# Loading the first token tiles as column halves over two queues, and q matmuls of the third token tile ahead of the first k matmuls

## The chip, the cores and the metric

The kernel runs on one core of one Trainium2 chip. Times are device microseconds (us), the median of several executions. "Span" is the time of the profiled execution from its first to its last instruction, about 1.7 us less than the run's time. PE is the TensorE matmul, PEld its weight load, DVE is VectorE, ACT ScalarE, POOL GpSimd, SP SyncE (here only an issuer of DMAs).

## The reference, cut to what matters

```python
x = A_x                                   # 1 x 2048 x 512, bf16
xn = _layernorm(x, axis=-1)               # 16 token tiles of 128 rows
return x + _A_ref(xn, A_wqkv, A_wo) + _B_ref(xn, B_w_in, B_w_sp, B_b_sp, B_w_out)
```

`_A_ref` is an attention over 8 dilated positions whose q, k, v come from `xn @ wqkv`; `_B_ref` is a gated MLP with a 2048 x 2048 mixing of the tokens. Everything starts from the normalised x, transposed so that the 512 channels lie on the partitions (`xnT`). Until the first tiles are loaded, normalised, transposed and copied, PE has nothing useful to do.

## The kernel before

The 16 token tiles are numbered 4 * tb + j. The first four to be worked on are tiles 0, 4, 8, 12 (j = 0); the text calls them **tile 0, 1, 2, 3** of the head. The loads, and the helpers:

```python
    def load_x0(E, tb, p0=0, p1=P):
        E.dma_start(xall[p0:p1, 0, tb, :], x2[tb * TBS + p0:tb * TBS + p1, :])
    ...
    load_x0(SP, 0, 0, 64)                 # tile 0: two partition halves
    load_x0(A, 0, 64, P)
    load_x0(A, 1)                         # tile 1: whole, on ACT's queue
    G.dma_start(xall[:, 0, 2:4, :], xblk[0][:, 2:4, :])     # tiles 2 and 3, by POOL
    load_wqk(SP, 0)                       # q weights
    SP.dma_start(xall[:, 1], xblk[1])     # x block 1
    load_wqk(SP, 1)                       # k weights
    ...
    def ln_stats(i):
        j, tb = i % 4, i // 4
        V.bn_stats(stats[:, i, :], xall[:, j, tb, :])
        V.bn_aggr(mv[:, i, :], stats[:, i, :])
    ...
    def qk_part(pq, j, m, b0, b1, ccs=(0, 1), p0=None):
        ...
        for cc in ccs:
            for kc in range(C):
                PE.matmul(pq[:, cc, ...], wqk[:, sd, kc, c0 + cc:D:C],
                          xv[:, kc, b0:b1, j, :], start=(kc == 0), stop=(kc == C - 1))
```

The head's schedule (order is by hand, each engine runs its instructions in the order written):

```python
    warm_up(10)                           # matmuls on zeros
    for n in range(2):
        ln_stats(t0[n]); ln_sqrt(col(t0[n]))
    for n in range(2):
        ln_tile(t0[n])                    # 1/x, then (x - mean) * rstd on DVE
        tr_copy(t0[n], tr(t0[n]))         # PE transposes into PSUM, ACT copies to xnT
    warm_up(1)
    warm_up(1, 2)
    ...                                   # statistics and normalisation of tiles 2, 3
    qk_part(pqs[0], 0, 0, 0, 2)           # q of tiles 0, 1
    tr_copy(t0[2], tr(t0[2]))
    qk_part(pqs[1], 0, 1, 0, 2, (0,))
    tr_copy(t0[3], tr(t0[3]))
    qk_part(pqs[1], 0, 1, 0, 2, (1,))
    qk_part(pqs[2], 0, 2, 0, 2)           # the first of k
```

The last group of output rows (o = 3) adds 16 x 4 matmuls of attention, eight row groups of 24-row matmuls on the tail channels of `uT`, and then the full ones:

```python
    def u_tr(n):                          # the last of 16: "T14", from SP
        SP.dma_start_transpose(uT[:, (n // 4) % 2, :, (n % 4) * P:(n % 4 + 1) * P], z1u[:, n % NZ1, :])
    ...
    def out_rest(o):                      # needs all four uT of its group
        for rt in range(2):
            for tb in range(TB):
                ...
                    PE.matmul(pc, uT[q:q + KR, o % 2, m, tb * P:(tb + 1) * P], wout[q:q + KR, m, cs], ...)
```

## Time and profile before

| | value |
|---|---|
| time | 204.58 us median of 3 (204.37 to 204.71) |
| span, granted clock | 202.8 us, 0.998 |
| PE busy | 97% |
| share of PE in the chain that ended last | 85% |
| first useful matmul (q) | 7.47 us |
| landings: tile 0, tile 1, tiles 2 and 3, q weights, x block 1, k weights | 3.35, 4.39, 5.16, 6.67, 8.17, 9.66 us |

The landings are the times of the last of a load's sixteen semaphore increments, from the trace's records.

With PE at 97% one reads where the other 3% are. The chain of waits of the first 10 us, start, length and what it was (SPq and ACTq are issues of DMAs):

```profile
0.81 0.56 ACTq L165
...
1.41 2.98 DMA r_x<-in_A_x_dram
...
4.41 0.71 DVE stats L203
...
5.14 0.18 DVE mv L204
...
5.41 0.42 DVE r_x L214
...
5.88 0.41 PE pt L221 x4
...
6.31 1.12 ACT xnT L225 x2
...
7.47 1.03 PE pq L306 x8
...
8.50 0.40 PE pt L221 x4
8.90 0.44 PE pq L306 x4
```

The reader is to see a single file of dependent steps: tile 1's load, its statistics, aggregation, normalisation of tile 0, transposes, two copies, q. After 7.47 the chain is PE's own work, with one small step: the transposes of tile 2 (8.50), which follow the q matmuls directly in this list, but started when DVE's normalisation ended (8.03 + 0.41), as the DVE timeline shows (start, busy, instruction):

```profile
4.17 0.18 DVE L204 BATCH_NORM_AGGREGATE mv<-stats 128x2 f32<-128x6 f32 x1
4.41 0.69 DVE L203 BATCH_NORM_STATS2 stats<-r_x 128x6 f32<-128x512 bf16 x1
5.14 0.18 DVE L204 BATCH_NORM_AGGREGATE mv<-stats 128x2 f32<-128x6 f32 x1
...
6.25 0.69 DVE L203 BATCH_NORM_STATS2 stats<-r_x 128x6 f32<-128x512 bf16 x1
...
8.03 0.41 DVE L214 TENSOR_SCALAR r_x<-r_x,mv,rstd 128x512 bf16<-128x512 bf16 x1
```

And the PE timeline of the last group's tail channels (L506) and full matmuls (L521):

```profile
194.23 0.38 PE L506 MATMUL po<-r_w,r_uz 24*128 24x512 bf16 x2
194.24 0.38 PE L506 MATMUL pa<-r_w,r_uz 24*128 24x512 bf16 x2
...
195.04 0.59 PE L521 MATMUL po<-r_w,r_uz 128*128 128x512 bf16 x2 [0.16 <-issue]
```

### The profile page before, as it was taken

Reading aid. Unit: us, or ns where it says so; the run is one execution under the profiler, and the core shown is the slowest. Engines: PE = TensorE matmul, PEld = TensorE weight load, DVE = VectorE, ACT = ScalarE, POOL = GpSimd, SP = SyncE. Lnnn points to the kernel's source line nnn. Section 1 sums busy time; section 2 is a strip of 40 time slices with the busy share of each in tenths; the row PEclk is TensorE's granted clock in tenths of the full one; section 3 lists DMA queues with packets and bytes.
Section 4 is the critical chain, followed back from the end, with each engine's and each line's share of the span. In section 5 each row is a group of like instructions: output and inputs, shape, how many; then the busy total and the mean of one; then the engine's idle time right before and its main releaser. Section 6 shows DMA issues by size and latency. Waiting matters only on the chain.

```text
span 202.8 us, 4061 instructions
## 1 busy us (share of the span) xinstructions
PE 196.2 (97%) x1679; PEld 125.0 (62%) x1683; DVE 185.0 (91%) x263; ACT 102.5 (51%) x163; POOL 18.0 (9%) x15
## 2 busy tenths in 40 slices
PE   7799999999999999999999999999999999999993
PEld 2689856555666666666566666666654644664561
DVE  4999799999999999999899999999999999988504
ACT  3575978978999986913733273595230010021000
POOL 5000000799200000000000000000000000000000
PEclk9999999999999999999999999999999999999999
DMA  5973448900000399149950975959910393574453
GB/s 146 353 264 73 96 94 253 198 1 3 0 0 3 87 157 206 44 87 239 220 123 21 204 135 118 231 138 162 207 42 3 97 174 89 140 203 94 116 184 103
DMA packets 65826, 25.91 MB, mean 128 GB/s; under 512 B 56208, under 2 KB 65488, under 8 KB 65552
## 3 DMA queue, kind: packets, MB, share of 16 engines
q1 hardware_dynamic: 65360, 25.12, 56.5%
q10 hardware_dynamic: 368, 0.27, 0.6%
q8 instruction: 13, 0.21, 0.5%
q0 software_dynamic: 80, 0.26, 0.4%
q14 instruction: 5, 0.04, 0.1%
HBM read 10.13 MB, written 2.10 MB: 60 GB/s over the span
## 4 chain that ended last, share of the span: by engine, by line
PE 85%; DMA 4%; SPq 3%; DVE 3%; issue 2%; ACT 1%; ACTq 0%; DVEq 0%
PE pg L449 35%; PE pz L235 19%; PE pq L306 13%; PE pv L410 7%; PE po L521 4%; PE po L497 4%; DMA r_x<-in_A_x_dram 1%; PE pl L360 1%; DMA r_uz<-r_uz 1%; DMA out_dram<-r_qk 1%; SPq L469 1%; DVE r_qk L511 1%; SPq L516 1%; SPq L474 1%; PE pt L221 1%
## 5 line engine op out<-in xcount | busy, mean ns | idle before, releaser
L449 PE MATMUL pg<-z,r_qk 128*128 128x344 bf16 x448 | 67.0, 309 | 0.0
L449 PEld LDWEIGHTS <-r_qk 128*128 128x128 bf16 x448 | 43.8, 98 | 21.8
L235 PE MATMUL pz<-w_z,xnT 128*128 128x344 bf16 x256 | 40.0, 309 | 0.0
L424 DVE TENSOR_TENSOR r_pr<-r_x,r_w 128x2048 bf16<-128x2048 bf16 x32 | 38.3, 1219 | 1.2 <-PE pl L360 0.8
L455 ACT ACTIVATE gs<-pg,b_col 128x688 bf16<-128x688 f32 x16 | 13.3, 830 | 41.3 <-PE pg L449 19.4
L428 DVE TENSOR_TENSOR r_pr<-r_pr 128x2048 bf16<-128x2048 bf16 x28 | 33.8, 1216 | 0.0
L235 PEld LDWEIGHTS <-xnT 128*128 128x128 bf16 x256 | 24.9, 98 | 13.4 <-issue 0.8
L306 PE MATMUL pq<-xnT,r_w 128*128 128x256 bf16 (+1 forms) x176 | 28.5, 316 | 0.3 <-ACT xnT L225 0.3
L340 DVE TENSOR_TENSOR r_pr<-r_qk 128x2048 bf16<-128x2048 bf16 x24 | 28.0, 1215 | 0.0
L306 PEld LDWEIGHTS <-r_w 128*128 128x128 bf16 x184 | 20.2, 114 | 7.5 <-issue 0.5
L297 ACT ACTIVATE r_uz<-pz 128x688 bf16<-128x688 f32 x16 | 11.7, 741 | 20.8 <-PE pz L235 20.6
L634 POOL CAST b_col<-b 128x16 f32<-128x16 bf16 x1 | 15.1, 15142 | 32.7 <-DMA b<-in_B_b_sp_dram 32.7
L316 ACT CAST r_qk<-pq 128x1024 bf16<-128x1024 f32 (+1 forms) x16 | 15.4, 990 | 4.4 <-PE pq L306 4.0
L521 PE MATMUL po<-r_w,r_uz 128*128 128x512 bf16 x66 | 14.9, 379 | 0.6 <-issue 0.6
L511 DVE TENSOR_TENSOR r_qk<-po,r_qk 128x512 bf16<-128x512 f32 x14 | 9.1, 684 | 6.8 <-DMA out_dram<-r_qk 5.1
L497 PE MATMUL po<-r_lg,r_pr 32*128 32x512 bf16 x224 | 14.5, 375 | 0.0
L410 PE MATMUL pv<-xnT,r_w 128*32 128x512 bf16 x256 | 14.4, 380 | 0.0
L521 PEld LDWEIGHTS <-r_uz 128*128 128x128 bf16 x85 | 8.0, 98 | 9.8 <-issue 1.5
L349 DVE TENSOR_TENSOR r_pr<-r_pr 128x4096 bf16<-128x4096 bf16 x6 | 13.6, 2286 | 0.0
L259 ACT ACTIVATE junk<-z 128x688 bf16<-128x688 bf16 x16 | 12.5, 780 | 0.1
L253 ACT ACTIVATE z<-pz 128x688 bf16<-128x688 f32 x16 | 11.7, 738 | 1.5 <-PE pz L235 1.5
L203 DVE BATCH_NORM_STATS2 stats<-r_x 128x6 f32<-128x512 bf16 x16 | 10.8, 672 | 1.7 <-DMA r_x<-in_A_x_dram 1.6
(82 smaller groups left out, 176.1 us busy)
## 6 DMA issues: line engine op xcount, KB each, us to landing
r_qk<-in_A_x_dram SPq DMA_DIRECT2D x16, 128.0 KB, 3.2
r_lg<-in_A_wo_dram SPq DMA_DIRECT2D x8, 256.0 KB, 4.6
out_dram<-r_qk SPq DMA_DIRECT2D x15, 128.0 KB, 1.8
r_w<-in_A_wqkv_dram SPq DMA_DIRECT2D x3, 512.0 KB, 4.6
r_x<-in_A_x_dram SPq DMA_DIRECT2D x3, 512.0 KB, 5.8
w_z<-in_B_w_in_dram SPq DMA_DIRECT2D x2, 688.0 KB, 5.4
r_w<-in_B_w_out_dram SPq DMA_DIRECT2D x1, 640.0 KB, 5.5
r_x<-in_A_x_dram POOLq DMA_DIRECT2D x1, 256.0 KB, 3.9
```

The source lines that it names most:

```text
L235: PE.matmul(pz[:, hh, 0:FHALF], xnT[:, kc, i * P:(i + 1) * P], wz[:, kc, hh * FHALF:(hh + 1) * FHALF], start=(kc == 0), stop=(kc == C - 1))
L306: PE.matmul(pq[:, cc, p0 * P:(p0 + b1 - b0) * P], wqk[:, sd, kc, c0 + cc:D:C], xv[:, kc, b0:b1, j, :], start=(kc == 0), stop=(kc == C - 1))
L316: cast = A.copy(dst, pq[:, :, p0 * P:(p0 + b1 - b0) * P].rearrange("p c (b t) -> p c b t", b=b1 - b0))
L340: prod = V.tensor_tensor(pr[g % 3][:, c].rearrange("p w b t -> p b w t"), q3.unsqueeze(2).broadcast_to([P, TB, 4, P]), k4, ALU.mult)
L349: V.tensor_tensor(pr[g % 3][:, 0:2], pr[g % 3][:, 0:2], pr[g % 3][:, 2:4], ALU.add)
L410: PE.matmul(pv[32 * tb:32 * tb + 32, dd, :], wv[:, kc, 2 * d2 + dd, :], xnT[:, kc, tb * TBS:(tb + 1) * TBS], start=(kc == 0), stop=(kc == ...
L424: V.tensor_tensor(pw_t[n], vp[:, :, off:off + P], a_sb[:, slot_w(w), ts].unsqueeze(1).broadcast_to([P, DH, P]), ALU.mult)
L428: V.tensor_tensor(pw_t[n] if dst is None else dst, pw_t[n], pw_t[m], ALU.add)
L449: PE.matmul(pg[:, hh, 0:FHALF], wsp[n][:, k, :], z2[:, k, hh * FHALF:(hh + 1) * FHALF], start=(k == 0), stop=(k == NT - 1))
L497: PE.matmul(pc, op[32 * tb:32 * tb + 32, d, o * P:(o + 1) * P], wo_r[32 * tb:32 * tb + 32, d, cs], start=(d == 8), stop=False, tile_positi ...
L521: PE.matmul(pc, uT[:, o % 2, m, tb * P:(tb + 1) * P], wout[:, m, cs], start=False, stop=(m == MCH - 3))
L634: G.tensor_copy(b_col[:], b16[:])
```

## The change

Its intent: tiles 0 and 1 come sooner and in column halves, so that statistics start on the first half; the second tile's copy is halved so that the first q matmuls (which take the channels two quarters at a time) start on the first half; and q matmuls of tile 2 fill PE while the k weights, now issued later, are still on their way.

```diff
-    stats = sb.tile([P, NT, 6], F32, name="stats")
+    stats = sb.tile([P, NT, 12], F32, name="stats")
...
-    def load_x0(E, tb, p0=0, p1=P):
-        E.dma_start(xall[p0:p1, 0, tb, :], x2[tb * TBS + p0:tb * TBS + p1, :])
+    def load_x0(E, tb, h):
+        E.dma_start(xall[:, 0, tb, 256 * h:256 * h + 256], x2[tb * TBS:tb * TBS + P, 256 * h:256 * h + 256])
...
-    load_x0(SP, 0, 0, 64)
-    load_x0(A, 0, 64, P)
-    load_x0(A, 1)
+    for tb in range(2):
+        load_x0(SP, tb, 0)
+        load_x0(A, tb, 1)
...
-    def ln_stats(i):
+    def ln_stats(i, parts=1):
         j, tb = i % 4, i // 4
-        V.bn_stats(stats[:, i, :], xall[:, j, tb, :])
-        V.bn_aggr(mv[:, i, :], stats[:, i, :])
+        w = D // parts
+        for h in range(parts):
+            V.bn_stats(stats[:, i, 6 * h:6 * h + 6], xall[:, j, tb, w * h:w * h + w])
+        V.bn_aggr(mv[:, i, :], stats[:, i, 0:6 * parts])
...
     for n in range(2):
-        ln_stats(t0[n])
+        ln_stats(t0[n], 2)
...
-        tr_copy(t0[n], tr(t0[n]))
+    tr_copy(t0[0], tr(t0[0]))
+    pt1 = tr(t0[1])
+    tr_copy(t0[1], pt1, 0, 2)
+    tr_copy(t0[1], pt1, 2, 4)
...
-    qk_part(pqs[0], 0, 0, 0, 2)
+    qk_part(pqs[0], 0, 0, 0, 2, kcs=range(2))
+    qk_part(pqs[0], 0, 0, 0, 2, kcs=range(2, 4))
...
     qk_part(pqs[1], 0, 1, 0, 2, (1,))
+    qk_part(pqs[0], 0, 0, 2, 3)
+    qk_part(pqs[1], 0, 1, 2, 3)
     qk_part(pqs[2], 0, 2, 0, 2)
...
-        qk_part(pqs[n], 0, n, 2, 4)
+        qk_part(pqs[n], 0, n, 3, 4)
```

Instruction by instruction, PE gets 16 weight loads and 16 matmuls more (3,398 instructions for 3,366, counted as twice the weight loads): 16 matmuls of 256 columns became 32 of 128. Nothing else is added but two statistics, one copy and one load.

More of the change, by code (lines that the diff above doesn't have):

```diff
@@ L222, in tr, with tr_copy @@
         return pt
-    def tr_copy(i, pt):
-        A.copy(xnT[:, :, i * P:(i + 1) * P], pt[:])
+    def tr_copy(i, pt, c0=0, c1=C):
+        A.copy(xnT[:, c0:c1, i * P:(i + 1) * P], pt[:, c0:c1, :])
     def tr_dma(i):
@@ L298, in z1_gelu, with qk_part @@
                      tiles.pop(("x", n))[:, :, 0:FHALF], ACT.Gelu_apprx_tanh)
-    def qk_part(pq, j, m, b0, b1, ccs=(0, 1), p0=None):
+    def qk_part(pq, j, m, b0, b1, ccs=(0, 1), p0=None, kcs=range(C)):
         sd, c0 = m // 2, 2 * (m % 2)
@@ L304, in qk_part @@
         for cc in ccs:
-            for kc in range(C):
+            for kc in kcs:
                 PE.matmul(pq[:, cc, p0 * P:(p0 + b1 - b0) * P], wqk[:, sd, kc, c0 + cc:D:C],
```

## The prediction

> **What bounds the kernel now.** One core, granted clock 0.998, median 204.58 us (204.37 to 204.71). The page has PE 97% busy; the chain of waits is 85% PE. From its first projection matmul at 7.47 us the PE runs almost without idle time to about 179 us (timeline). So the change can shorten only the head: the time before 7.47 us, and the gap at 8.34 to 8.50, where the transposes of the third tile wait for the DVE's normalisation. The rest should only slide.
>
> **The head, by the chain and the timeline.** ACT issues tile 1 at 1.41, it lands at 4.39; DVE statistics 4.41, aggregation 5.14, first normalisation 5.41, transposes 5.88, two ACT copies from 6.31 (585 ns each), matmul 7.47. Tile 0 came as two partition halves issued together at 0.81; the semaphore records show them full at 2.97 and 3.35; its statistics ran 3.45 to 4.14. The q weights landed at 6.67, x block 1 at 8.17, the k weights at 9.66, with DMA at about 350 GB/s from 4 us on.
>
> **What the change does.**
> - Loads: four 64 KB column halves, so the first half's statistics run while the second lands. The Trainium skill ("DMA: Bandwidth & Descriptors", Rules for kernel authors) says that transfers to disjoint partition halves serialize; 2.97 and 3.35 agree, and I expect column halves to do likewise. Tile 1 comes ahead of the weights on both queues. Rows shrink from 1024 to 512 bytes: twice the packets, which costs some of the gain.
> - Statistics: two 256-wide instructions instead of one of 690 ns: an estimate of 0.42 us each, starting 0.33 apart (VectorE at 0.96 GHz: the Trainium skill, "Trainium Kernel Development and Optimization", NeuronCore Architecture). With both halves there it costs 0.07 us; with halves apart it saves up to 0.3. My estimate: tile 1's aggregation starts at 4.95 (4.75 to 5.15) instead of 5.14, and normalisations and transposes shift with it.
> - Copy in halves: 372 ns each (estimated from 585 at 512 columns, 1012 at 1024), so the first q matmul could start another 0.2 us earlier, near 7.0. But the q weights are issued 0.6 us later and may land at 6.7 to 7.2, and what is won here waits at the third tile's transposes, which the DVE sets. Little by itself.
> - Order: 16 matmuls of 256 columns (109 ns apart) become 32 of 128 (transposes of that width are 56 ns apart): +0.04 us. They put 0.9 us before the first k matmul, so that later k weights (9.7 to 10.3) don't stall it.
>
> **On the critical path**: 0.2 us off the third tile's transposes (8.50 to about 8.3), kept to the end. Predicted 204.35 us, 80% range 203.9 to 204.8; faster by over 2%: 0.01, within 2%: 0.98, slower: 0.01.
>
> **What would show it.** Tile 0's statistics starting near 3.1; tile 1's aggregation near 4.95; first q matmul at 7.0 to 7.3, PE still waiting for the DVE before the third tile's transposes; k matmuls at about 10.9 without a wait; PE continuous afterwards, every later stage 0.2 earlier.
>
> **What would make it wrong.** The 512-byte rows landing so late that the DVE starts no earlier; q weights landing past 7.3; 128-column matmuls slower than 56 ns apart (their weights are strided: 0.8 us more if they took 80); a later wait (block 1 of x past 8.6, the transposing DMAs) that takes the gain back.

## More of the kernel before

From the page, engine use and the chain by engine (busy us, share, instructions; then shares of the span):

```profile
PE 196.2 (97%) x1679; PEld 125.0 (62%) x1683; DVE 185.0 (91%) x263; ACT 102.5 (51%) x163; POOL 18.0 (9%) x15
...
q8 instruction: 13, 0.21, 0.5%
...
PE 85%; DMA 4%; SPq 3%; DVE 3%; issue 2%; ACT 1%; ACTq 0%; DVEq 0%
```

## The result, and the profile after

The changed kernel took 204.56 us (median of 4, 204.38 to 204.61), the kernel before 204.50 in the same comparison (4 runs): ratio 1.000, 95% interval 0.9983 to 1.0018. The span is 202.9 us for 202.8.

The head did become faster, and by more than forecast at first. The DVE timeline after (the lines that answer to those above):

```profile
2.94 0.75 DVE L205 BATCH_NORM_STATS2 stats<-r_x 128x6 f32<-128x256 bf16 x2 [1.12 <-DMA r_x<-in_A_x_dram]
3.73 0.21 DVE L206 BATCH_NORM_AGGREGATE mv<-stats 128x2 f32<-128x12 f32 x1
3.85 0.70 DVE L205 BATCH_NORM_STATS2 stats<-r_x 128x6 f32<-128x256 bf16 x2
4.58 0.21 DVE L206 BATCH_NORM_AGGREGATE mv<-stats 128x2 f32<-128x12 f32 x1
...
6.07 0.69 DVE L205 BATCH_NORM_STATS2 stats<-r_x 128x6 f32<-128x512 bf16 x1 [0.28 <-DMA r_x<-in_A_x_dram]
...
7.86 0.41 DVE L216 TENSOR_SCALAR r_x<-r_x,mv,rstd 128x512 bf16<-128x512 bf16 x1
```

Tile 1's aggregation starts at 4.58 instead of 5.14, 0.56 us earlier, but tile 2's normalisation at 7.86 only 0.17 us earlier: its statistics waited at 6.07 for the load of tiles 2 and 3, which landed at 6.05 instead of 5.16. PE's side of the same stretch, from the list of waits (waiter, what it waited for, us in total, times, longest):

```profile
PEld L308 <- DMA r_w<-in_A_wqkv_dram: 1.0, 1, 1.0
...
PE pq L308 <- ACT rstd L209: 0.5, 1, 0.5
```

The first q matmul started at 7.36. The second line blames ACT, but ACT's own list has nothing that PE needs then: the weight load just before that matmul waited for the q weights (first line), which landed at 7.32. A matmul and its weight load wait separately, and both lines have to be read.

From 9.3 us on, PE was continuous and 0.14 to 0.18 us earlier than before: the transposes of tile 2 at 8.33 (before 8.50), the first matmul of the MLP at 22.35 (22.49), the first of the token mixing at 76.69 (76.83), the first tail-channel matmul of the last group at 194.09 (194.23). From the PE timelines, the transposes after (8.33) and the first matmuls of the MLP after and before:

```profile
8.33 0.40 PE L223 MATMUL pt<-ident,r_x 128*128 128x128 bf16 x4
...
22.35 3.66 PE L237 MATMUL pz<-w_z,xnT 128*128 128x344 bf16 x24
...
22.49 3.66 PE L235 MATMUL pz<-w_z,xnT 128*128 128x344 bf16 x24
```

In the last group the gain was lost. PE timeline, list of waits, and DMA queues in the stretch 192.0 to 193.6 us (packets, MB, share of 16 engines):

```profile
194.09 0.38 PE L508 MATMUL po<-r_w,r_uz 24*128 24x512 bf16 x2
194.47 0.39 PE L508 MATMUL pa<-r_w,r_uz 24*128 24x512 bf16 x2
...
195.24 0.38 PE L523 MATMUL po<-r_w,r_uz 128*128 128x512 bf16 x1 [0.16 <-issue]
```

```profile
PEld L508 <- DMA r_uz<-r_uz: 0.5, 1, 0.5
```

```profile
q1 hardware_dynamic: 527, 0.22, 59.0%
q8 instruction: 1, 0.02, 4.1%
```

After its first two matmuls the last group waits for a transposing DMA, until 194.47. Before, the same matmuls followed at once (194.24), and the same DMA queues between 192.0 and 193.5 us had no packet of queue 8:

```profile
q1 hardware_dynamic: 658, 0.24, 69.8%
```

(That trace's own last packet of queue 8 began at 193.56, after the DMA had landed.)

The trace's semaphore records tell more of this DMA, the last of the sixteen that transpose u (T14). Its sixteen increments came between 192.89 and 193.03 before. After, fifteen came by 192.89 and the sixteenth at 194.43. The Trainium skill ("DMA: Bandwidth & Descriptors", Why a DMA increments its semaphore by 16 and not by 1) says that each of up to sixteen engines posts one increment when its own data has landed; so one engine of sixteen was 1.5 us late. And a 16,384-byte packet of queue 8 ran from 192.33 to 193.39 us, while T14 was moving. The Trainium skill ("Runtime: NRT & Kernel Launch", Instruction fetch mechanics) says that an engine's sequencer refills its instructions by its own DMA queue in 16 KiB blocks, 256 instructions each. This agrees with that: thirteen such packets in each trace, an estimate of 13 x 256 = 3,328 instructions, beside PE's 3,366, and no other engine has more than a few hundred. That page also calls the cost "mostly hidden". Here it was not, if the following theory holds. There was slack, but not enough: before, T14 had landed at 193.03 and the first matmul that needs it ran at 194.24, 1.2 us later.

**Theory 1.** The change adds 32 PE instructions. They move the blocks in which PE's instructions are fetched, and the last fetch now falls on the last transposing DMA, whose slowest engine then holds up PE for about 0.35 us. That takes the head's gain back. **Rival A:** the late DMA was chance, a matter of that one execution. **Rival B:** it comes with the head's earlier timing or the new loads, not with the number of instructions. Open besides: which part of the change makes the head's gain, and why it was only 0.14 us after 0.56 us at the aggregation.

### The profile page after: what moved, and what is told of

The parts are those of the page before. It is cut to its first block, busy times and chain, and to the rows that moved or that the text cites. A ratio compares the mean times of both kernels' runs of the same rounds, so it can differ in the third digit from the quotient of the medians. Undisturbed runs are those within 1.5% of the kernel's fastest.

```text
span 202.9 us, 4098 instructions
## 1 busy us (share of the span) xinstructions
PE 197.4 (97%) x1695; PEld 125.2 (62%) x1699; DVE 185.3 (91%) x265; ACT 102.6 (51%) x164; POOL 18.0 (9%) x15
## 4 chain that ended last, share of the span: by engine, by line
PE 87%; SPq 3%; DVE 2%; issue 2%; DMA 2%; ACT 1%; DVEq 0%
PE pg L451 35%; PE pz L237 19%; PE pq L308 13%; PE pv L412 7%; PE po L523 4%; PE po L499 4%; PE pwm L550 2%; SPq L476 1%; PE pl L362 1%; DMA r_uz<-r_uz 1%; DVE r_qk L513 1%; SPq L471 1%; DMA out_dram<-r_qk 1%; PE pt L223 1%; SPq L518 1%
## 5 line engine op out<-in xcount | busy, mean ns | idle before, releaser
L308 PE MATMUL pq<-xnT,r_w 128*128 128x256 bf16 (+2 forms) x192 | 28.6, 304 | 0.5 <-ACT rstd L209 0.5
L412 PEld LDWEIGHTS <-r_w 128*32 128x32 bf16 x256 | 9.4, 138 | 4.5 <-issue 0.3
```

The costliest lines, as they stand in the source:

```text
L308: PE.matmul(pq[:, cc, p0 * P:(p0 + b1 - b0) * P], wqk[:, sd, kc, c0 + cc:D:C], xv[:, kc, b0:b1, j, :], start=(kc == 0), stop=(kc == C - 1))
L412: PE.matmul(pv[32 * tb:32 * tb + 32, dd, :], wv[:, kc, 2 * d2 + dd, :], xnT[:, kc, tb * TBS:(tb + 1) * TBS], start=(kc == 0), stop=(kc == ...
```

## The experiments

Twelve runs, timed against the kernel before on the same chip. The kernel before itself was spread over 204.46 to 206.64 us on these chips (single executions over 1 us off the median occurred in it and in two of the variants, shift_only and after_far_act; their cause was not studied).

| run | median us (range, runs) | before on the same chip | ratio (95% interval) |
|---|---|---|---|
| before_again | 204.84 (1) | 204.84 (204.50 to 205.80, 11) | - |
| after_again | 204.36 (204.28 to 204.55, 6) | the same | 0.9974 (0.9955 to 0.9993) |
| shift_only | 205.19 (204.88 to 206.36, 6) | the same | 1.0023 (0.9997 to 1.0049) |
| loads_only | 204.69 (204.46 to 205.48, 6) | the same | 0.9995 (0.9971 to 1.0020) |
| order_only | 204.96 (204.80 to 204.99, 6) | 204.82 (204.46 to 206.64, 11) | 0.9995 (0.9967 to 1.0022) |
| after_far | 204.39 (204.21 to 204.51, 6) | the same | 0.9969 (0.9941 to 0.9996) |
| before_far | 205.37 (204.96 to 205.78, 6) | the same | 1.0024 (0.9993 to 1.0054) |
| after_far_act | 205.06 (203.90 to 205.22, 6) | the same | 0.9988 (0.9956 to 1.0021) |
| after_third | 204.36 (204.26 to 204.68, 6) | 204.66 (204.51 to 205.19, 11) | 0.9985 (0.9973 to 0.9997) |
| whole_copy | 204.52 (204.30 to 204.80, 6) | the same | 0.9991 (0.9978 to 1.0003) |
| after_split3 | 204.13 (203.95 to 204.32, 5) | the same | 0.9971 (0.9960 to 0.9983) |
| after_split3_w | 204.01 (203.86 to 204.15, 5) | the same | 0.9965 (0.9953 to 0.9977) |

And what the fourteen traces show of the tail: PE's instructions (twice the weight loads), the last fetch, the increments of T14's semaphore, and the time from the last group's first tail-channel matmul to the start of its last full matmul, which is 4.82 us if nothing waits.

| trace | PE instructions | last fetch, us | T14: 15th, 16th increment | first tail-channel to last full matmul |
|---|---|---|---|---|
| before | 3,366 | 193.56 to 194.45 | 193.02, 193.03 | 4.82 |
| before_again | 3,366 | 192.93 to 194.38 | 193.05, 193.06 | 4.82 |
| loads_only | 3,366 | 193.31 to 194.73 | 193.23, 193.28 | 4.83 |
| after | 3,398 | 192.33 to 193.39 | 192.89, 194.43 | 5.17 |
| after_again | 3,398 | 192.06 to 193.09 | 192.60, 194.12 | 5.15 |
| after_third | 3,398 | 192.01 to 193.06 | 192.56, 194.09 | 5.15 |
| order_only | 3,398 | 192.50 to 193.51 | 193.02, 194.54 | 5.14 |
| shift_only | 3,398 | 192.93 to 193.99 | 193.43, 195.04 | 5.23 |
| whole_copy | 3,398 | 192.05 to 193.07 | 192.58, 194.10 | 5.15 |
| before_far | 3,434 | 192.15 to 193.32 | 194.69, 194.70 | 5.31 |
| after_far | 3,466 | 189.28 to 190.61 | 193.07, 193.11 | 4.82 |
| after_far_act | 3,466 | 189.93 to 191.22 | 193.80, 193.81 | 4.82 |
| after_split3 | 3,462 | 188.83 to 190.10 | 192.56, 192.59 | 4.82 |
| after_split3_w | 3,462 | 188.61 to 189.82 | 192.55, 192.58 | 4.82 |

The mark is not found at T14 alone. The fourteen traces hold 364 transposing DMAs of x and u. In fourteen of them the sixteenth increment came more than 0.4 us after the fifteenth (1.52 to 1.82 us), and in each of these a fetch had begun 0.42 to 0.59 us before the fifteenth. Only one other had a fetch begin at that distance, and it was on time. Two of the fourteen are in the kernel before, near 120 us, where PE did not wait: a late increment costs time only where its consumer has less slack than that.

### 1. The two kernels again

No edit; a second and a third profile.

> The kernel before, unchanged, for a second profile. Theory 1 (the added PE instructions move a 16 KB instruction fetch onto the last transposing DMA): last 16 KB fetch again near 193.6 us, the rest-columns matmuls of the last output group (24 rows) start near 194.2 without a wait, span near 202.8. Rival (the collision is chance, different from run to run): the fetch stands elsewhere by a microsecond or more. In both, landings of tile 1 near 4.4, the q weights near 6.7, tiles 2 and 3 near 5.2.

> The change, unchanged, for a second profile and a closer ratio. Theory 1: landings repeat (tile 1 near 3.5, tiles 2 and 3 near 6.0, the q weights near 7.3), the body is again 0.14 us earlier than before, the last 16 KB fetch is again near 192.3 and the last output group waits about 0.35 us; ratio 0.9995 to 1.001. Rival (chance): the tail wait is missing in this profile, and five rounds show the head's gain, ratio 0.999 to 0.9995.

> The changed kernel a third time, beside the runs below on one chip. Expected from the two profiles so far: tile 1's aggregation at 4.6 to 4.9, third tile's transposes 8.0 to 8.35, last fetch at 192 to 192.5, the last output group waits 0.35 us; median 204.35 to 204.6.

The tail repeats in each: the late sixteenth increment in all three profiles of the change, in neither of the kernel before. So the wait is not the chance of one execution: rival A falls. The fetch stands within 0.7 us from profile to profile of one kernel; in before_again it came at 192.93, not near 193.6 as expected, just as T14 landed, and did no harm.

The head is another matter. In both new profiles it gained more than in the first: transposes of tile 2 at 8.04 and 8.00 (8.33 in the first, 8.50 and 8.54 before). Tiles 2 and 3 landed at 5.37 and 5.29 (6.05), the q weights at 6.71 and 6.87 (7.32). The first profile of the change had the unlucky landings. after_again's expectation that the body would be 0.14 us earlier was therefore too small: its first MLP matmul is at 22.06, 0.43 us earlier than before, of which the tail takes 0.33. The ratios 0.9974 and 0.9985 are clear of 1, by 0.26 and 0.15 per cent; the first comparison showed no gain (1.000), and its interval reaches down to 0.9983. PE's share of this is small: its last full matmul starts at 198.95 and 198.92, 0.10 and 0.13 us earlier than before (199.05). The rest of the shorter spans (202.56 in both, for 202.84 and 203.12 of the kernel before) lies behind it: in the two traces of the kernel before, the last additions on DVE had waited for an output DMA and ended 0.52 and 0.76 us after PE's last matmul, in the three of the change 0.43. So the kernel before lost time of its own at the end, which sets off part of the tail's loss.

### 2. Only the PE instructions, nothing else

```diff
-    warm_up(10)
+    warm_up(4)
+    warm_up(2, 2)
+    warm_up(20, 1)
```

The same 5,120 columns of warm-up in 26 matmuls, on the kernel before: 32 PE instructions more.

> The kernel before, with the ten warm-up matmuls cut into 26 of the same 5120 columns, so that PE runs 32 instructions more, as the change adds, and nothing else is different. Theory 1: the head is unchanged (first q matmul near 7.47, third tile's transposes near 8.50), the last fetch moves to about 192.3 and the last output group waits 0.3 to 0.4 us: ratio 1.001 to 1.002. Rival: no shift of the tail, ratio within 0.0005 of 1.

The tail waits (5.23 us instead of 4.82), with the same mark: fifteen increments by 193.43, the sixteenth at 195.04. So neither the new loads nor an earlier head is needed: rival B falls. The time agrees in direction but is not clear of 1, and its head was not as expected either: in this profile tile 1 landed at 4.79 instead of 4.39, and the tile 2 transposes came at 8.91. That part of its loss came with the later landing. Landings differ between traces of one kernel too, so one trace cannot lay it to the 32 instructions.

### 3. Only the order of the q matmuls

The kernel before, with `qk_part(pqs[0], 0, 0, 2, 3)` and `qk_part(pqs[1], 0, 1, 2, 3)` ahead of the first of k, and `qk_part(pqs[n], 0, n, 3, 4)` later.

> The kernel before with only the q matmuls of token tile 2 ahead of the first of k (32 PE instructions more, loads and statistics as before). The head can't gain: third tile's transposes at 8.5, body later by the 0.04 us of the narrower matmuls. If the added instructions put the last 16 KB fetch on the last transposing DMA: fetch near 192.3, the last output group waits 0.35 us, ratio 1.001 to 1.002. If that wait in the three kernels with 32 more instructions so far was something else in the head: no wait, ratio 1.000 to 1.0005.

As expected in the trace: transposes of tile 2 at 8.48, no gain; the tail waits. Its PE timeline and waits there:

```profile
194.24 0.38 PE L506 MATMUL po<-r_w,r_uz 24*128 24x512 bf16 x2
194.59 0.38 PE L506 MATMUL pa<-r_w,r_uz 24*128 24x512 bf16 x2
```

```profile
PEld L506 <- DMA r_uz<-r_uz: 0.4, 1, 0.4
```

The first line stands where it stood before the change (194.23); the second is 0.35 us later. The time itself is inconclusive: 204.96 for 204.82 by medians, 0.9995 by means, because one run of the kernel before took 206.64.

### 4. Only the loads and the split statistics

The change with the whole copy of tile 1 and the old order of q and k; PE has the 3,366 instructions of before.

> The change without the copy in halves and without the q matmuls of token tile 2 ahead: column halves and split statistics alone, PE has as many instructions as before. Landings as in the changed kernel (tile 1 near 3.5, k weights near 10.3). Expected: third tile's transposes at 8.3 to 8.5, then the first k matmul, due near 9.7, waits for the k weights until about 10.35, so the body is 0.4 to 0.6 us later than before; the last fetch near 193.6 and no wait in the tail under theory 1: ratio 1.002 to 1.003. If the order of the q matmuls is not needed, ratio 0.999.

No wait in the tail, as theory 1 says. In the head the transposes of tile 2 came at 8.14, 0.36 us earlier than before, and then PE waited for the k weights, which landed at 10.00:

```profile
10.05 1.17 PE L308 MATMUL pq<-xnT,r_w 128*128 128x256 bf16 x9 [0.41 <-DMA r_w<-in_A_wqkv_dram]
```

So the loads make the head's gain, and the new order is what keeps it: with the loads alone the first MLP matmul is at 22.73, later than before (22.49). The loss was 0.24 us rather than the 0.4 to 0.6 expected, as the k weights came earlier than in the first profile of the change (10.33). The expected ratio of 1.002 to 1.003 was not seen: 0.9995, with an interval up to 1.002. The loads alone lose 0.24 us in the body, the order alone gains nothing there (first MLP matmul at 22.50); together they gain 0.14 to 0.46 us.

### 5. Moving the fetch further

If it matters where the fetch falls, more instructions should help where 32 hurt. All warm-up matmuls are cut to 128 columns, on the change and on the kernel before:

```diff
-    warm_up(10)
+    warm_up(40, 1)
...
-    warm_up(1)
-    warm_up(1, 2)
+    warm_up(6, 1)
```

> The changed kernel with its warm-up matmuls cut to 128 columns each, the same columns in total, 68 PE instructions more than the change. If the tail's wait comes from where the fetch falls, the last fetch moves to about 189.5 to 190.5, before the last transposing DMA moves its data (191.5 to 192.9), the rest-columns matmuls of the last group run without a wait, and 0.3 us of the head's gain stays: ratio 0.996 to 0.9975 and median near 204.1. If not: a wait of 0.35 us as in the change, ratio as the change's.

> Control: the kernel before with the same cut of the warm-up matmuls, 68 PE instructions more than before. If only the number of added instructions counted, the tail would wait longer than with 32; if where the fetch falls counts, the last fetch is near 191 and either just clears the last transposing DMA (no wait, ratio 0.9995 to 1.0005) or just touches it (wait under 0.4 us, ratio up to 1.002). Head as before: transposes of tile 3 near 8.5.

after_far: the last fetch moved to 189.28, all sixteen increments came together, and the tail's wait is gone (4.82), with 100 instructions more than before. But the median, 204.39, is not the 204.1 expected. The gain was lost elsewhere, by the same mark:

```profile
26.06 2.11 PE L308 MATMUL pq<-xnT,r_w 128*128 128x512 bf16 x9 [0.16 <-DMA xnT<-r_x]
```

Another fetch had moved as well, from 28.70 in the change to 23.47 (until 24.39). There the transposing DMAs of x run: of one of them fifteen increments came by 23.91 and the sixteenth at 25.50, and the next landed at 25.92, after PE wanted it. From the first MLP matmul to the first v matmul took 19.56 us, for 19.23 to 19.25 in all traces but this one and after_far_act, which carries the same cut (19.46; fetch at 24.20, sixteenth increment at 26.23): 0.33 us again. A fetch on these DMAs does not always cost time: in the change the fetch at 28.70 also made a sixteenth increment late (29.18, then 30.72), and PE did not wait.

before_far failed its expectation in number: its last fetch came at 192.15, not near 191, and the tail waited 0.49 us. There all sixteen increments of T14 were late (194.57 to 194.70), not one. This form is found elsewhere too: in after_third, order_only, whole_copy and after_split3_w a transposing DMA of x, issued at 26.36 to 26.89, had a fetch begin 1.25 to 1.81 us after its issue, and all its increments were late (the first 3.81 to 4.10 us after the issue, 2.29 to 2.35 in the traces with only a late sixteenth, whose fetch began 1.96 to 2.09 us after the issue). In before_far the fetch began 1.73 us after T14's issue at 190.42, in the six traces with 3,398 instructions 2.04 to 2.09. So the form goes with where the fetch begins; by what mechanism is open. It agrees with theory 1 in that a fetch near 192 goes with a late T14, and it is the reason not to guess a fetch's place from the count alone: 68 more instructions put it where 32 do.

### 6. Tiles 2 and 3 from ACT's queue

after_far with one more edit, since the statistics of tile 2 had waited for this load in the first profile:

```diff
-    G.dma_start(xall[:, 0, 2:4, :], xblk[0][:, 2:4, :])
+    A.dma_start(xall[:, 0, 2:4, :], xblk[0][:, 2:4, :])
```

> after_far with the load of x tiles 2 and 3 issued third on the ACT queue instead of POOL. If the third tile's statistics wait for that load because it is issued by POOL and its packets come last (landing 6.05 and 5.37 in the two profiles of the change): landing before 5.0, statistics of the third tile directly after the second normalisation (about 5.8), its transposes near 8.0, q weights near 6.7 to 7.3; ratio 0.9945 to 0.9965. If all loads only share the same rate: no gain over after_far within 0.1 us, q weights later than 7.

A miss. The load came later, not sooner: complete at 6.68, after the q weights (6.54), where POOL's had landed at 5.09 in after_far. Transposes of tile 2 at 8.97, PE idle 1.06 us before them. The Trainium skill ("DMA: Bandwidth & Descriptors", Issuing engines are not separate DMA queues) says that all issuers share the same sixteen engines and that issuing from several saves only issue time. This run agrees so far that the load gained nothing by it and x block 1 landed at 8.12 (7.96 in after_far). That it lost its place by being issued third, at 1.73 instead of 1.30, is the likely reading and not shown. The trace is of one execution, 204.97; the six ran from 203.90 to 205.22, so the landing may differ in others.

### 7. The second tile's copy whole again

```diff
-    tr_copy(t0[1], pt1, 0, 2)
-    tr_copy(t0[1], pt1, 2, 4)
+    tr_copy(t0[1], pt1)
```

> The change with the second tile copied whole again. If the third tile's transposes wait for the DVE in any case, as the prediction says, the first q matmul moves later by up to 0.25 us and nothing else changes: ratio to the change within 0.0005 (0.1 us). If the halved copy carries part of the gain: 0.2 us slower than the change. The last fetch and the tail's wait as in the change, since PE has the same instructions.

The first q matmul was at 7.14 (6.91 in the change on that chip), but it waited for the q weights, which landed at 7.09, and the transposes of tile 2 came at 8.04 for 8.00. No part of the gain hangs on the halved copy in this trace. The times, 204.52 and 204.36, overlap and don't separate the two.

### 8. A version that keeps the gain

The instructions that move the last fetch are now put behind the second fetch: the matmuls of 512 columns of q and k of x block 3 (`j == 3`; "token tile 3" in the text below), near 36 to 52 us, are cut in two.

```diff
-        qk_part(tiles["q", j, m], j, m, 0, TB)
+        if j == 3:
+            qk_part(tiles["q", j, m], j, m, 0, 2)
+            qk_part(tiles["q", j, m], j, m, 2, TB)
+        else:
+            qk_part(tiles["q", j, m], j, m, 0, TB)
```

> The change with the 32 matmuls of 512 columns that make q and k of token tile 3 (near 36 to 52 us) cut into 64 of 256: 64 PE instructions more than the change, but after the second fetch, which stays near 28.5, clear of the transposing DMAs of 22.5 to 30 us that the warm-up cut ran into (26.06). If the fetch theory holds for both places: no PE wait near 26 us, last fetch near 189.5, no wait of the last output group, cost of the narrower matmuls 0.1 us; so 0.2 to 0.3 us faster than the change, median near 204.1. Rival (the two fetch effects don't account for it): same as the change or slower by 0.1.

The second fetch stayed at 28.44, the last moved to 188.83. Against the expectation it was not clear of the transposing DMAs: one of x had its sixteenth increment at 30.70, 1.82 us after the fifteenth. But nothing waited for it. No wait near 26 us, and none in the tail:

```profile
193.79 0.38 PE L512 MATMUL po<-r_w,r_uz 24*128 24x512 bf16 x2
193.80 0.38 PE L512 MATMUL pa<-r_w,r_uz 24*128 24x512 bf16 x2
...
194.60 1.03 PE L527 MATMUL po<-r_w,r_uz 128*128 128x512 bf16 x4 [0.16 <-issue]
```

Median 204.13, against 204.36 for the change on the same chip (0.23 us less), with 64 instructions more. The same cuts would be useless as an optimisation by themselves: they are there only to shift the fetch. The last run adds one edit, the q weights in two DMAs by halves of their rows, for the first four q matmuls need the first half alone:

```diff
-    load_wqk(SP, 0)
+    for kh in range(2):
+        SP.dma_start(wqk[:, 0, 2 * kh:2 * kh + 2],
+                     A_wqkv[256 * kh:256 * kh + 256, 0:D].rearrange("(k p) f -> p k f", p=P))
```

> after_split3 with the q weights loaded by two DMAs, the first half of the contraction rows first, as the first four q matmuls need only those. If a late q weight load limits the head (7.32 in one profile of the change): first q matmul steady near 6.8 to 6.9 and third tile's transposes set by the DVE (8.0 to 8.2). If the DVE sets it anyway: within 0.1 us of after_split3.

The halves landed at 6.03 and 6.78, the first q matmul was at 6.68 (6.76), and the transposes of tile 2 at 7.94, exactly as without: the DVE sets them. Median 204.01, ratio 0.9965 (0.9953 to 0.9977), the fastest of all kernels tried and 0.65 us under the kernel before on that chip. Whether the last 0.12 us are the halves' doing is not settled: the intervals overlap.

## Why the prediction was right or wrong

The number held: 204.56 lies in 203.9 to 204.8, and "within 2%" was right. That is partly luck: the range also holds the kernel before (204.50), and the gain of 0.2 us was not there in that comparison. The reasoning was right in outline and failed in the step that carried the gain to the end.

- **"The change can shorten only the head."** Right of the intent; incomplete. The change also lengthened the tail, by 0.33 to 0.35 us in its three traces (0.32 to 0.41 in all six with 3,398 PE instructions). The prediction had followed PE only to about 179 us.
- **"Tile 1's aggregation starts at 4.95 (4.75 to 5.15)."** Mis-sized. It measured 4.58, 4.66 and 4.42. The prediction names no landing for tile 1; with a half on each queue ahead of the weights it landed at 3.50 to 3.58 (4.39 before), which is where the extra gain came from. The term for two statistics instead of one was right: the pair took 0.70 to 0.75 us for 0.69.
- **"I expect column halves to do likewise"** (to serialize). The halves of tile 0 landed 0.21 us apart (2.91 and 3.12), less than the partition halves of before (2.97 and 3.35). The skill's sentence, cited in the prediction, is on partition halves: here both pairs landed one after the other, by less than half a microsecond, and no run shows how far they serialize.
- **"Normalisations and transposes shift with it."** Wrong in the first profile: 0.56 us at the aggregation became 0.17 at tile 2, because the load of tiles 2 and 3 landed at 6.05. I named block 1 of x as a risk, not this load. In the two later profiles of the change it landed in time and the transposes came at 8.00 to 8.04.
- **"PE still waiting for the DVE before the third tile's transposes."** Not in the first profile, where the late q weights (7.32) kept PE busy until then; in after_again yes, a gap of 0.21 us.
- **"Little by itself"** of the halved copy: supported, transposes 8.04 without it and 8.00 with it.
- **"+0.04 us" for the narrower matmuls:** right; they are 56 ns apart in the trace, strided weights or not.
- **"So that later k weights don't stall it":** right, shown by its absence: without the q matmuls ahead PE waited 0.41 us; with them the first k matmul ran at 10.55 without a wait, the weights having landed at 10.33.
- **"Kept to the end": the step that failed.** The body was 0.14 us earlier until 194 us in the first profile (0.43 and 0.46 in the others), and then the last group waited 0.33 to 0.35 us for T14. The runs put the cause in the 32 added PE instructions: adding them alone makes the wait (shift_only, order_only), leaving them out removes it (loads_only), and adding still more in the right place removes it too (after_far, after_split3). That it is the instruction fetch that delays one share of the transposing DMA is shown by coincidence (fourteen late sixteenth increments, each with a fetch that had begun 0.42 to 0.59 us before the fifteenth) and by moving the fetch: the mark at T14 was then gone. The trace does not say on which of the sixteen engines a fetch ran, so the collision on one engine is the best reading, not itself shown.

What stays open: why loads of the same kernel land up to 0.8 us apart from run to run (tiles 2 and 3: 5.29 to 6.05), which makes the head's gain vary between 0.14 and 0.46 us and is larger than most edits here; and why a fetch that begins somewhat earlier makes all sixteen increments late, as in before_far, instead of one.

## What to carry to other kernels

When a PE-bound kernel gains in its head and nothing at its end, slide along the trace and find where the shift is lost; here the number of instructions alone moved an instruction fetch onto a DMA that PE waits for, and the traces show it as one late semaphore increment of sixteen. A DMA with little slack before its consumer (1.2 us here) is the weak place, and it can be spared by moving the fetch (instructions added or dropped in a place of one's choice, then checked, since the place can't be guessed from the count) or, which no run here tried, by issuing that DMA earlier. The small loads that start the chain gained here by going ahead of the large ones on both queues; then what waits is the next load in line, and it has to be given work in front of it.

## What the Trainium skill lacked or had wrong

- "Runtime: NRT & Kernel Launch", Instruction fetch mechanics: the blocks of 16 KiB agree (13 packets of 16,384 bytes per execution). It calls their cost mostly hidden and does not say that they delay data DMAs. Here a block took 0.88 to 1.83 us in the fourteen traces, and one falling on a transposing DMA went with a sixteenth increment 1.52 to 1.82 us late in fourteen cases and, at the end of the kernel, with a wait of PE of 0.32 to 0.41 us, in 204.
- No page gives this as something to look for when an edit changes only the number of instructions: 32 PE instructions more cost PE 0.32 us at the end of the kernel (order_only), 0.41 us where nothing but the warm-up was cut (shift_only).
- "DMA: Bandwidth & Descriptors", Latency and other measured facts: it has about 0.6 us to the first byte for loads issued from SP and ACT. In the trace of before, the first packets of tile 0's half from ACT ran at 2.17 us, 1.36 us after the start of their issue and 0.80 us after its end; the page does not say from which moment it counts.
